# A fused attention and feed-forward kernel: the first k and q loads follow each other without gates, the first v load begins at once, the other early v loads get gates of their own, and fewer tiles are transposed on TensorE

## The chip, the cores and the metric

The kernel runs on one core of a Trainium2 chip. The metric is the device time of one execution in microseconds (us), and lower is better. A run is called slow when it is more than 1.5% above the fastest run of the same kernel; verdicts use fast runs alone. A trace is of one profiled execution, and its span is about 1.7 us shorter than the device time of the same run.

## The reference

```python
def _attn_ref(q, k, v, n_global, n_local):       # q, k, v: 4 batches x 8 heads x 768 x 64, float32
    ...
    keep = is_global | is_local                   # first 8 positions, or the last 96
    scores = scale * q @ k.T + bias[None]         # bias: -slope(head) * distance
    a = softmax over the kept positions
    return a @ v

def _moe_ref(x, w_in, w_out):                     # x: 3072 x 512, w_in: 512 x 2048, w_out: 2048 x 512
    h = x @ w_in
    g = h - np.tanh(h)
    return g @ w_out
```

The attention output is rearranged to x (3072 rows of 512) and goes through the feed-forward part. The result is 3072 x 512 in float32.

## The kernel before

The 3072 rows are 24 tiles of 128, numbered u = 0 to 23, six for each batch. For each tile the kernel loads k, q and v, transposes k and q (**T**), computes scores, exponentials and masks, multiplies by v (**AV**), normalizes (**x**), transposes x, and runs the first product (**m1**, with w_in), tanh, a subtraction, and the second product (**m2**, with w_out).

A small planner inside the kernel, at build time, gives each operation an assumed duration and picks, step by step, what can start first. What it emits is a fixed order for each engine. Changing an assumption or a gate therefore also changes the order of the instructions, on every engine. This matters below.

There are two roads for loads. GpSimd issues those that also convert to bf16: k and q of tiles 0 to 3 (128 KB each as written) and the eight pieces of the weights (512 KB each). These go through its ring (software queue). SyncE issues all v and the k and q of later tiles, as float32 (256 KB each), which an engine then casts. The DMA transposes of later tiles and the stores are also in SyncE's order.

```python
    PE_T, PE_X = 9, 9        # tiles below these are transposed on TensorE (k and q; x), others by DMA
    EARLY, EARLY2 = 9, 5
    ...
    def started(key, i):
        dmas[key] = i
        g = gate_of.get(key)
        if g is not None:            # a gate: issue this load only when load g has landed
            tc.add_manual_dep(i.ins, dmas[g].ins.name, ...)
    ...
    def load(u, nm, src, dst):
        ...
        if u < LB and nm != "vf":    # LB = 4
            started(("ld", nm, u), nc.gpsimd.dma_start(out=kq[u][...], in_=...))      # L161
        else:
            started(("ld", nm, u), nc.sync.dma_start(out=dst[u], in_=...))            # L166
    def load_w_in(j):
        started(("in", j), nc.gpsimd.dma_start(out=w_in_bf[j], ...))                  # L170
    def load_w_out(j):
        started(("out", j), nc.gpsimd.dma_start(out=w_out_bf[j], ...))                # L173
    ...
    def cast_v(u):                                                                    # L185
        nc.gpsimd.tensor_copy(out=vb[u % NV][:, :, 0:Dh], in_=vf.pop(u))
    ...
    AHEAD = 5.0              # how many tiles transposes may run ahead of m1
    before = [               # the order of loads: tiles ("t": k, q, v) and weight pieces
        ("t", 0), ("t", 1), ("t", 2), ("t", 3), ("in", 0), ("in", 1), ("in", 2), ("in", 3), ("out", 0),
        ("out", 1), ("out", 2), ("t", 4), ("out", 3), ("t", 5), ("t", 6), ("t", 7),
    ]
    ...
    for n, (key, ring, us) in enumerate(atoms):          # atoms: the single loads of that list
        if n and ring is not atoms[n - 1][1]:            # where the ring changes,
            due = at + 0.3 - T_LAND - T_ISSUE[ring]
            past = [x for e, x in ends if e <= due]
            if past:
                gate_of[key] = past[-1]                  # wait for the last load that is due by then
            elif key[1] == "vf":
                gate_of[key] = ("ld", "kf", key[2])
        at += us
        ends.append((at, key))
```

The gates that come out of this are: v0 after k0; v1 and k2 after q0; v2 and k3 after q1; v3 and w_in piece 0 after q2; k4 after w_out piece 1; w_out piece 3 after piece 2; k5 after v4.

The softmax here doesn't subtract the row's maximum and nothing guards it: scores larger than these inputs give would overflow.

Of the kernel before, what the change touches and what calls it, by code (L numbers as in the profile page):

```python
# [12 lines left out]
ENG = mybir.EngineType  # L13
# [3 lines left out]
def kernel(  # L17
# [11 lines left out]
    nc = tc.nc  # L29

    B, H, S, Dh = q.shape
# [15 lines left out]
    NV = 8  # L47
    PE_B = 4
    LB = 4
    PE_T, PE_X = 9, 9  # L50
    HT = 3


    EARLY, EARLY2 = 9, 5
    groups = [[u] for u in range(EARLY)] + [[u, u + 1, u + 2] for u in range(EARLY, NU, HT)]
    group_of = {u: g for g, us in enumerate(groups) for u in us}

# [22 lines left out]
    vb = [cpool.tile([P, H, Dh + 1], BF16, name=f"vb{i}") for i in range(NV)]  # L80
# [40 lines left out]
        nc.scalar.activation(mk[:, h, :, :], rmat, AF.Exp, bias=0.0, scale=-slope(h))  # L121


    ops = {}
    w_in_r = moe_w_in.rearrange("(c p) f -> p c f", p=P)
    w_out_r = moe_w_out.rearrange("(j p i) d -> j p i d", p=P, i=FJ)
    PE, ACT, DVE, POOL, SP = ENG.PE, ENG.Activation, ENG.DVE, ENG.Pool, ENG.SP

    LAT = {PE: 0.17, ACT: 0.1, DVE: 0.1, POOL: 0.12, SP: 0.0}

    def op(key, eng, us, fn, after=(), take=(), give=(), pri=0, dma=0.0):
        ops[key] = dict(
            key=key, eng=eng, us=us, fn=fn, after=[a for a in after if a is not None],
            take=list(take), give=list(give), pri=pri, dma=dma,
        )

    gate_of = {}
# [13 lines left out]
    kf, qf, vf = {}, {}, {}  # L151
# [23 lines left out]
    def cast(u, j, src):  # L175
        if u not in kq:
            kq[u] = bpool.tile([P, 2, H * Dh], BF16, name="kq")
        t = src.pop(u)
        nc.gpsimd.tensor_copy(  # L179
            out=kq[u][:, j, :].rearrange("p (c a d) -> p a c d", a=2, d=Dh),  # L180
            in_=t.rearrange("p (a c) d -> p a c d", a=2),
        )

    def cast_v(u):
        nc.gpsimd.tensor_copy(out=vb[u % NV][:, :, 0:Dh], in_=vf.pop(u))  # L185


    tr, qk, sc, pr, av, xs, xT = {}, {}, {}, {}, {}, {}, {}
# [121 lines left out]
    def shape1(g):  # L310
        n = len(groups[g]) * P
        return groups[g][0] // HT, groups[g][0] % HT * P, n, 512 // n
# [69 lines left out]
    def store(u):  # L382
        nc.sync.dma_start(out=out[u * P : (u + 1) * P, :], in_=ots.pop(u))


    AHEAD = 5.0
    WARM = (1.3, 13.0)
    BEGUN = {("ld", "kf", 0): 3.1, ("ld", "qf", 0): 3.8}
    T_LD, T_LD8, T_ST, T_DT, T_DX = 1.15, 0.75, 0.7, 1.75, 0.9
    T_W = {"in": 3.15, "out": 2.65}  # L390
    before = [
        ("t", 0), ("t", 1), ("t", 2), ("t", 3), ("in", 0), ("in", 1), ("in", 2), ("in", 3), ("out", 0),
        ("out", 1), ("out", 2), ("t", 4), ("out", 3), ("t", 5), ("t", 6), ("t", 7),
    ]


# [2 lines left out]
    T_LAND, T_ISSUE = 1.0, {SP: 1.6, POOL: 2.0}  # L399
    atoms = []  # L400
    for it in before:
        if it[0] == "t":
            u = it[1]
# [3 lines left out]
        else:  # L407
            atoms.append((it, POOL, T_W[it[0]]))
    at = 2.6
    ends = []  # L410
    for n, (key, ring, us) in enumerate(atoms):
        if n and ring is not atoms[n - 1][1]:
            due = at + 0.3 - T_LAND - T_ISSUE[ring]
            past = [x for e, x in ends if e <= due]
            if past:
                gate_of[key] = past[-1]
            elif key[1] == "vf":
                gate_of[key] = ("ld", "kf", key[2])
        at += us
        ends.append((at, key))  # L420
    for u in range(NU):
# [6 lines left out]
    for key, ring, us in atoms:  # L428
        gate = [gate_of.get(key), last.get(ring) and ("issue", last[ring])]
        if key[0] == "ld":  # L430
            nm, u = key[1:]
# [12 lines left out]
    for g, us in enumerate(groups):  # L444
        b, o, n, m = shape1(g)
# [7 lines left out]
    for u in range(NU):  # L453
        i = u % NQ
        if u >= LB:
            op(("ck", u), POOL, 0.62, lambda u=u: cast(u, 1, kf), after=[("ld", "kf", u)], take=["kq"], give=["kf"], pri=-1)
            op(("cq", u), POOL, 0.62, lambda u=u: cast(u, 0, qf), after=[("ld", "qf", u), ("ck", u)], give=["qf"], pri=-1)
        op(("cv", u), POOL, 0.62, lambda u=u: cast_v(u),
           after=[("ld", "vf", u), ("AV", u - NV + 1) if u >= NV else None,
                  ("V", (u - NV) // NQ * NQ + NQ - 2) if u >= NV else None], give=["vf"])  # L460
        go = [key for a, key in prog if a <= u - AHEAD]
        before_T = [("issue", ("T", u - 1)) if u else None, go[-1] if go else None]
# [41 lines left out]
    for g, us in enumerate(groups):  # L504
        b, o, n, m = shape1(g)
# [31 lines left out]
    def plan():  # L537
        bufs = {"big": 2, "one": 4, "mo": 3, "kf": 4, "qf": 4, "vf": 4, "kq": 4, "p0": 3, "p1": 3,
                "x": 3, "xT": 4, "g": 3, "th": 3, "ot": 4}
        avail = {n: [0.0] * c for n, c in bufs.items()}  # L540
        free = {PE: WARM[0], ACT: 4.9, DVE: 5.0, POOL: 3.3, SP: 0.7}
        avail["one"][0] = WARM[1]
        dma_free = 0.0
# [73 lines left out]
    def with_warm(order):  # L617
        pe = sorted(t for t, key in order if ops[key]["eng"] is PE)
        last = WARM[0]
        n = 0  # L620
        for t in pe:
            while True:
                us = 0.43 if last < 4.8 else 0.22
                if last + us + 0.08 > min(t, WARM[1]):
                    break
# [55 lines left out]
```

## Time and profile before

| | kernel before |
|---|---|
| device time, median of 3 (lowest to highest) | 221.76 us (220.97 to 223.07) |
| span of the profiled run | 221.1 us |
| TensorE work, counted at the spacings that the chain shows | 200.5 us |
| time lost on TensorE before 40 us, and after | 10.8 us, 6.0 us |
| eviction and store after the last matmul | 3.8 us |
| clock halved | once, 12.36 to 15.78 us |

The prediction shows how the work is counted and which lines carry it. "Time lost" is everything on TensorE's time line that is not this work: idle time, and the excess of matmuls at half the clock. The split at 40 us is mine; by then the start is over in both kernels. The last matmul's end is counted at the same spacings; by its recorded end the tail is 3.5 us, as the prediction has it.

One more view is used later. The DMA view of the kernel before, for 0 to 40 us in slices of 1 us, shows the busy share of the DMA engines in tenths; then comes the row of the table of stretches for the same 40 us (window, length, busy us of PE, PEld, DVE, ACT, POOL, clock, DMA share, GB/s):

```profile
DMA  0039989999999959999999999999999989299989
```

```profile
0.00:40.00 40.00, 36.84 (x556) 26.18 (x560) 21.47 (x55) 25.30 (x40) 14.11 (x29) 0.96 0.98 178
```

The reader is to see one short dip at 14 us and another at 34. The transfers are kept fed for nearly all of the first 40 us, at 178 GB/s.

### The profile page before, as it was taken

What the parts mean: (1) busy time and instruction counts of PE and PEld (TensorE: products, weight loads), DVE (VectorE), ACT (ScalarE), POOL (GpSimd) and SP (SyncE); (2) the same over time, 40 slices, a digit from 0 to 9 for tenths busy, and PEclk for the clock granted to TensorE, in tenths of its full rate; (3) what the DMA queues carried; (4) which work ended last, traced back from release to release, by engine and by line L of the source; (5) the groups of instructions that cost most, each with busy time, mean ns of one, the idle gap of its engine ahead of it and who ended that gap; (6) DMA issues with size and microseconds to landing.
All of it is one profiled execution on the core that took longest, in us unless ns stands there. A gap on an engine that the chain in (4) does not pass through costs nothing.

```text
span 221.1 us, 5458 instructions
## 1 busy us (share of the span) xinstructions
PE 211.7 (96%) x2208; PEld 137.7 (62%) x2233; DVE 128.7 (58%) x258; ACT 129.2 (58%) x209; POOL 56.6 (26%) x98
## 2 busy tenths in 40 slices
PE   7699999999999989999999999999999999999993
PEld 2356996557998767556655665566666655555552
DVE  6136773357899677525885767557767644444300
ACT  4467766575887675445766656558684554534320
POOL 6473003146174345332144423330000000000000
PEclk9969999999999999999999999999999999999999
DMA  4999998599999999999999999997124121001112
GB/s 59 206 174 207 213 209 174 129 226 251 209 215 213 177 185 236 198 227 215 214 221 220 220 182 209 244 227 154 24 63 96 49 71 47 14 35 50 47 50 94
DMA packets 98025, 34.56 MB, mean 156 GB/s; under 512 B 91216, under 2 KB 94544, under 8 KB 98000
## 3 DMA queue, kind: packets, MB, share of 16 engines
q1 hardware_dynamic: 94160, 28.98, 63.8%
q0 software_dynamic: 3840, 5.24, 14.0%
q8 instruction: 17, 0.28, 0.5%
q14 instruction: 8, 0.07, 0.1%
HBM read 27.26 MB, written 6.29 MB: 152 GB/s over the span
## 4 chain that ended last, share of the span: by engine, by line
PE 80%; DMA 14%; issue 1%; SPq 1%; POOL 1%; ACT 1%; DVE 0%; POOLq 0%; ACTq 0%
PE one L352 34%; PE one L325 31%; DMA kf<-in_k_dram 6%; PE big L242 5%; DMA qk<-kq 4%; DMA kq<-in_k_dram 3%; PE big L265 2%; PE big L269 2%; PE big L235 2%; PE one L364 2%; DMA kq<-in_q_dram 1%; PE one L194 1%; SPq L209 1%; PE one L201 1%; PE one L292 1%
## 5 line engine op out<-in xcount | busy, mean ns | idle before, releaser
L342 DVE TENSOR_TENSOR g<-one,th 128x384 bf16<-128x384 f32 (+1 forms) x116 | 67.5, 595 | 35.4 <-ACT th L336 32.7
L336 ACT ACTIVATE th<-one 128x384 f32<-128x384 f32 (+1 forms) x116 | 60.6, 526 | 44.5 <-PE one L325 43.1
L352 PEld LDWEIGHTS <-g 128*128 128x128 bf16 x368 | 34.2, 98 | 33.8
L250 ACT ACTIVATE pd<-big 128x1024 bf16<-128x1024 f32 x24 | 24.6, 1023 | 12.8 <-PE big L242 12.8
L325 PE MATMUL one<-xT,w_in_bf_100 128*128 128x128 bf16 (+1 forms) x224 | 25.3, 258 | 0.0
L325 PE MATMUL one<-xT,w_in_bf_99 128*128 128x128 bf16 (+1 forms) x224 | 24.9, 258 | 0.0
L325 PE MATMUL one<-xT,w_in_bf_97 128*128 128x128 bf16 (+1 forms) x224 | 24.5, 258 | 0.0
L325 PE MATMUL one<-xT,w_in_bf_98 128*128 128x128 bf16 (+1 forms) x224 | 24.2, 258 | 0.1
L179 POOL CAST kq<-kf 128x512 bf16<-128x512 f32 x20 | 13.6, 680 | 40.5 <-DMA kf<-in_k_dram 40.1
L380 ACT COPY ot<-one 128x512 f32<-128x512 f32 x23 | 13.5, 587 | 17.1 <-PE one L352 16.9
L352 PE MATMUL one<-w_out_bf_101,g 128*128 128x512 bf16 x85 | 22.8, 379 | 0.5 <-issue 0.2
L352 PE MATMUL one<-w_out_bf_102,g 128*128 128x512 bf16 x88 | 22.9, 380 | 0.2
L250 ACT ACTIVATE po<-big 128x1024 bf16<-128x1024 f32 x20 | 20.5, 1024 | 4.1 <-PE big L242 4.1
L352 PE MATMUL one<-w_out_bf_104,g 128*128 128x512 bf16 x87 | 22.4, 379 | 0.3
L352 PE MATMUL one<-w_out_bf_103,g 128*128 128x512 bf16 x84 | 22.1, 380 | 0.3
L325 PEld LDWEIGHTS <-w_in_bf_99 128*128 128x128 bf16 x224 | 17.5, 114 | 5.7
L325 PEld LDWEIGHTS <-w_in_bf_98 128*128 128x128 bf16 x224 | 17.6, 114 | 5.3
L254 DVE TENSOR_TENSOR pd<-pd,mk 128x1024 bf16<-128x1024 bf16 x20 | 15.1, 756 | 9.5 <-ACT pd L250 9.5
L325 PEld LDWEIGHTS <-w_in_bf_97 128*128 128x128 bf16 x224 | 17.3, 114 | 5.0
L325 PEld LDWEIGHTS <-w_in_bf_100 128*128 128x128 bf16 x224 | 17.0, 114 | 5.3
L242 PEld LDWEIGHTS <-qk 64*128 64x128 bf16 x352 | 10.0, 95 | 11.9 <-issue 8.6
L242 PE MATMUL big<-qk 64*128 64x128 bf16 x352 | 16.1, 220 | 1.2 <-DMA qk<-kq 1.0
(108 smaller groups left out, 199.0 us busy)
## 6 DMA issues: line engine op xcount, KB each, us to landing
vf<-in_v_dram SPq DMA_DIRECT2D x24, 256.0 KB, 5.0
out_dram<-ot SPq DMA_DIRECT2D x23, 256.0 KB, 2.9
kf<-in_k_dram SPq DMA_DIRECT2D x20, 256.0 KB, 3.8
qf<-in_q_dram SPq DMA_DIRECT2D x20, 256.0 KB, 4.6
kq<-in_k_dram POOLq DMA_DIRECT2D x4, 128.0 KB, 4.8
kq<-in_q_dram POOLq DMA_DIRECT2D x4, 128.0 KB, 5.1
w_in_bf_97<-in_moe_w_in_dram POOLq DMA_DIRECT2D x1, 512.0 KB, 5.4
w_in_bf_98<-in_moe_w_in_dram POOLq DMA_DIRECT2D x1, 512.0 KB, 7.2
```

What stands on the lines that cost most here:

```text
L179: nc.gpsimd.tensor_copy(out=kq[u][:, j, :].rearrange("p (c a d) -> p a c d", a=2, d=Dh), in_=t.rearrange("p (a c) d -> p a c d", a=2),)
L235: nc.tensor.matmul(s[:, a * NP : (a + 1) * NP, :], ident, bm[:, a * NP : (a + 1) * NP, m, :], start=True, stop=False,)
L242: nc.tensor.matmul(s[:, hh * NP + p, :], qk[u - o][r, 1, p, :], qk[u][r, 0, p, :], start=(u >= PE_B), stop=(u >= PE_B or p == NP - 1),)
L250: nc.scalar.activation(pr[u, o], s, AF.Exp, bias=0.0, scale=scale)
L254: nc.vector.tensor_tensor(out=pr[u, o], in0=pr[u, o], in1=mk[:, :, m, :], op=ALU.mult)
L265: nc.tensor.matmul(dst, pr[u, 0][:, h, :], vb[u % NV][:, h, :], start=True, stop=last,)
L269: nc.tensor.matmul(dst, pr[u, 1][:, h, :], vb[(u - 1) % NV][:, h, :], start=False, stop=True,)
L325: nc.tensor.matmul(t[:, (f - f0) * n : (f - f0 + 1) * n], w_in_bf[j][:, c, i : FJ * P : FJ], xT[b][:, c, o : o + n], start=(c == 0), stop= ...
L336: nc.scalar.activation(h_view(ths[g, f0], g), h_view(hs[g, f0], g), AF.Tanh, bias=0.0, scale=1.0)
L342: nc.vector.tensor_tensor(out=gs[b][:, f0 : f0 + m, o : o + n], in0=h_view(hs.pop((g, f0)), g), in1=h_view(ths.pop((g, f0)), g), op=ALU.su ...
L352: nc.tensor.matmul(os_[u], gs[u // HT][:, f, t * P : (t + 1) * P], w_out_bf[f // FJ][:, f % FJ, :], start=(f == 0), stop=(f == CF - 1),)
L380: nc.scalar.copy(out=ots[u], in_=os_.pop(u))
```

## The change

The intent is to let GpSimd issue its first loads back to back, to begin the first v in the empty first microseconds, to bring w_in piece 0 forward, and to leave fewer transposes to TensorE. The diff, cut to its core:

```diff
-    PE_T, PE_X = 9, 9
+    PE_T, PE_X = 8, 5
-    EARLY, EARLY2 = 9, 5
+    EARLY, EARLY2 = 9, 3
-    def cast_v(u):
-        nc.gpsimd.tensor_copy(out=vb[u % NV][:, :, 0:Dh], in_=vf.pop(u))
+    def cast_v(u, e=POOL):
+        (nc.vector if e is DVE else nc.gpsimd).tensor_copy(out=vb[u % NV][:, :, 0:Dh], in_=vf.pop(u))
-    AHEAD = 5.0
-    WARM = (1.3, 13.0)
+    AHEAD = 6.0
+    WARM = (1.3, 15.0)
-    T_LD, T_LD8, T_ST, T_DT, T_DX = 1.15, 0.75, 0.7, 1.75, 0.9
-    T_W = {"in": 3.15, "out": 2.65}
+    T_LD, T_LD8, T_ST, T_DT, T_DX = 1.1, 0.65, 0.7, 1.75, 0.9
+    T_W = {"in": 2.6, "out": 2.6}
     before = [
-        ("t", 0), ("t", 1), ("t", 2), ("t", 3), ("in", 0), ("in", 1), ("in", 2), ("in", 3), ("out", 0),
-        ("out", 1), ("out", 2), ("t", 4), ("out", 3), ("t", 5), ("t", 6), ("t", 7),
+        ("t", 0), ("t", 1), ("t", 2), ("in", 0), ("t", 3), ("in", 1), ("t", 4), ("in", 2), ("in", 3),
+        ("t", 5), ("out", 0), ("out", 1), ("out", 2), ("out", 3), ("t", 6), ("t", 7),
     ]
...
-    for n, (key, ring, us) in enumerate(atoms):
-        if n and ring is not atoms[n - 1][1]:
-            ...
+    by = None
+    for key, ring, us in atoms:
+        beside = key[:2] == ("ld", "vf") and key[2] < LB
+        if beside and key[2]:
+            gate_of[key] = ("ld", "vf", 0) if key[2] == 1 else ("ld", "kf", key[2] - 2)
+        elif not beside:
+            if by not in (None, ring):
+                ...                      # the gate as before, over the loads that are not "beside"
+            by = ring
...
-        op(("cv", u), POOL, 0.62, lambda u=u: cast_v(u),
+        op(("cv", u), (DVE, POOL) if u < LB else (POOL,), (0.48, 0.62) if u < LB else (0.62,), lambda e, u=u: cast_v(u, e),
```

The gates after the change are: v0 none; v1 after v0; v2 after k0; v3 after k1; k4 after v3; w_in piece 2 after piece 1; k5 after w_in piece 2; w_out piece 0 after w_in piece 3; k6 after w_out piece 2. GpSimd's ring holds k0, q0, k1, q1, k2, q2, w_in 0, k3, q3, w_in 1 with no gate among them. `T_LD` to `T_W` are the planner's assumed times of transfers. `WARM` bounds the stretch in which the planner fills idle time of TensorE with warm-up multiplications of zeros.

More of the change, by code (lines that the diff above doesn't have):

```diff
@@ L121, in mask @@
         nc.scalar.activation(mk[:, h, :, :], rmat, AF.Exp, bias=0.0, scale=-slope(h))
+    PE, ACT, DVE, POOL, SP = ENG.PE, ENG.Activation, ENG.DVE, ENG.Pool, ENG.SP
     ops = {}
@@ L126 @@
     w_out_r = moe_w_out.rearrange("(j p i) d -> j p i d", p=P, i=FJ)
-    PE, ACT, DVE, POOL, SP = ENG.PE, ENG.Activation, ENG.DVE, ENG.Pool, ENG.SP
     LAT = {PE: 0.17, ACT: 0.1, DVE: 0.1, POOL: 0.12, SP: 0.0}
@@ L410 @@
     ends = []
-    for n, (key, ring, us) in enumerate(atoms):
-        if n and ring is not atoms[n - 1][1]:
-            due = at + 0.3 - T_LAND - T_ISSUE[ring]
-            past = [x for e, x in ends if e <= due]
-            if past:
-                gate_of[key] = past[-1]
-            elif key[1] == "vf":
-                gate_of[key] = ("ld", "kf", key[2])
+    by = None
[5 more added lines that the diff above has]
+            if by not in (None, ring):
+                due = at + 0.3 - T_LAND - T_ISSUE[ring]
+                past = [x for e, x in ends if e <= due]
+                if past:
+                    gate_of[key] = past[-1]
+            by = ring
         at += us
```

## The prediction

> **What bounds the kernel now.** I read four views of the profile: the page, then the chain of waits, then the table of stretches, then the timelines of TensorE and GpSimd over the first 36 us. On the page TensorE is busy nearly throughout, DMA works at its limit to about slice 28, and the clock row has one dip:
>
> ```profile
> PE 211.7 (96%) x2208; PEld 137.7 (62%) x2233; DVE 128.7 (58%) x258; ACT 129.2 (58%) x209; POOL 56.6 (26%) x98
> ...
> PEclk9969999999999999999999999999999999999999
> DMA  4999998599999999999999999997124121001112
> ```
>
> Busy is not useful, so I count TensorE's work from spacings that the chain shows. Sixteen 128-wide first-product matmuls (L325) take 0.89 us, four 384-wide ones 0.65, four of the second product (L352) 0.86, sixteen scores (L242) 0.55, a pair of bias matmuls (L235) 0.43, sixteen 64-wide transposes (L201) 0.44, eight wide transposes (L194) 0.45, four of x (L292) 0.22, the last 32 (L364) 3.5, and AV 0.031 each. With the program's counts (576, 320, 368, 352, 14, 128, 40, 36, 32, 352) this is 32.0+51.9+79.3+12.1+3.0+3.5+2.2+2.0+3.5+10.9 = **200.4 us**. The trace shows only 344 of the 368 L352 matmuls; I use the program's count. The last matmul ends at 217.5, so 17.1 us are lost on TensorE, and 3.5 us of eviction and store follow to 221.1.
>
> When is it lost? The first L325 starts at 20.07. Before it there are 128 L201, 12 L235, 48 L242, 40 AV and 8 L292, that is 3.5+2.6+1.65+1.25+0.45 = 9.4 us of work. So **10.7 us are lost before 20.07 and 6.4 us in the 197 us after**. The chain of waits names the early loss:
>
> ```profile
> 2.01 3.02 DMA kq<-in_q_dram
> 5.03 0.28 issue
> 5.32 5.54 DMA kq<-in_k_dram
> 10.90 0.44 PE one L201 x16
> ```
>
> The reader sees k of tile 2 issued only once q of tile 0 landed (5.03: a gate), then 5.54 us of transfer, and TensorE starting on it at 10.90. The GpSimd timeline shows the two gates inside the ring:
>
> ```profile
> 5.32 0.51 POOL L161 DMA_DIRECT2D kq<-in_k_dram  x1 [1.18 <-DMA kq<-in_q_dram]
> ...
> 8.20 0.52 POOL L161 DMA_DIRECT2D kq<-in_k_dram  x1 [1.85 <-DMA kq<-in_q_dram]
> ```
>
> The table of stretches (columns: window and length; busy us of PE, PEld, DVE, ACT, POOL; then clock, DMA share, GB/s) shows what the hole did:
>
> ```profile
> 5.00:10.00 5.00, 4.00 (x78) 2.17 (x75) 0.69 (x1) 2.67 (x4) 2.69 (x5) 1.00 1.05 189
> 10.00:15.00 5.00, 4.10 (x65) 2.44 (x66) 1.75 (x4) 2.19 (x3) 2.81 (x4) 0.74 1.00 180
> 15.00:20.00 5.00, 4.98 (x96) 2.79 (x96) 2.53 (x7) 3.92 (x5) 3.60 (x7) 0.92 1.21 200
> ```
>
> From 12.36 to 15.78 the clock was halved, right after TensorE idled 8.96 to 10.90. Note also that DMA is already busy from 5 us: removing gates mostly reorders transfers rather than filling an idle DMA.
>
> **What the Trainium skill says.** (1) "TensorE: Matmul & The Clock Gate", Part 1, says an idle activity window of about 3.4 us drops the clock to half. The trace agrees on size (one dip of 3.41 us at 0.5), though 1.94 us idle within a window was enough. (2) "DMA: Bandwidth & Descriptors", Issuing engines are not separate DMA queues: transfers from GpSimd and SyncE interleave on the same 16 engines. The trace agrees: v of tile 0, moving while GpSimd's ring was mostly empty, took 1.3 us from first to last packet; v of tiles 1 and 2, beside k and q, took 2.5 and 2.7; v of tile 4, beside a w_out piece, took 5.1. (3) Same page, Anatomy of one DMA: a fixed cost of about 2 us. The trace's first k took 3.07 us from issue to landing with packets moving for only 1.16. (4) The clock-gate page's architectural detail says VectorE is strict FIFO; this matters for the moved v casts, and no run so far tests it here.
>
> **The change, part by part.**
>
> *Less TensorE work.* PE_T 9 to 8 takes 8 wide transposes away, 8 x 0.056 = 0.45 us; PE_X 9 to 5 takes 16 x transposes, 0.90 us. The instruction order shows the score groups in 18 single and 13 double runs, where 26 and 9 were before: four joins. A single run takes 0.33 and a double 0.55 in the chain, so a join saves 0.11, together 0.44. All of this lies on the bounding engine: **-1.8 us**. In exchange DMA gets one more qk and four more x transposes. A recorded qk transpose moves packets for 1.0 to 1.4 us when undisturbed and an x one for 0.7, so 1.2 + 4 x 0.7 = 4 us of DMA in the 50 to 90 us region, where DMA is full. But tile 5 now loads before w_out, and AHEAD 6 lets transposes go further ahead, so I count this as zero.
>
> *The first loads.* In the new order GpSimd issues k1, q1, k2, q2, w_in piece 0, k3, q3, w_in piece 1 without a landing gate; at about 0.5 us an issue k2 goes out at 4.1 (5.32 before). v0 goes out at about 0.8 instead of 4.44, and uses DMA before the first k's packets at 2.72; it should land near 4 to 5, and may delay k0 by 0.3. A k or q piece takes about 0.7 us of packets when alone (128 KB at some 180 KB/us) and 1.3 to 1.7 beside a v. I work it out serially: q1 done near 7.3, k2 8.6, q2 10.0, plus about 0.8 to landing: k2 lands near 9.4 (10.86), q2 10.8 (11.76). w_in piece 0 follows and lands near 14 (18.15), but k3 and q3 stand behind it: near 15.7 and 17 (13.72, 14.50). v1 lands near 8.5 (12.14), v2 near 11 (13.86), v3 near 13.6.
>
> *What TensorE makes of it.* T(2) starts 1.5 us earlier and the 2 us hole shrinks, so the halved clock (1.7 us lost, half of 3.41) probably does not return whole. But the order then has m1 of tile 0 ahead of AV(1), T(3) behind k3 and q3, and the second quarter of m1 behind w_in piece 1, near 20. By 20.4 I count 3.5 (T) + 2.15 (bias) + 1.4 (scores) + 1.25 (AV) + 0.45 (x) + 1.8 (two m1 quarters) = 10.5 us done, so 9.9 lost instead of 10.7: **-0.8 us**.
>
> *The v casts of tiles 0 to 3 on VectorE.* 4 x about 0.48 (the planner's figure) where GpSimd took 0.61 to 0.71. GpSimd is then free to issue; VectorE was busy 2.44 of 10 us from 5 to 15. The work is hidden, but cast 2 stands ahead of the first normalization, so a late v2 holds x(0).
>
> *Order and gates after 20 us.* w_in pieces 2 and 3 wait for piece 1 to land, tile 5 for piece 2, w_out for piece 3. GpSimd's order has cast v5 between cast k5 and cast q5, so T(5) waits for v5, which moves beside w_out as v4 did. I allow **+1.0 us**. The other stalls after 20 us (6.4, among them 0.96 at 81.2 and 0.42 at 108.8 behind qk transposes) fall by a guess of 1.6 with more slack: **-1.6**.
>
> *Sum.* -1.8 - 0.8 + 1.0 - 1.6 = -3.2 us on a profiled 221.1, which gives 217.9, and as a median **218.5**.
>
> **The rivals.** *A: transfers only change places.* DMA moves the same bytes and was busy from 5 us (share 1.05, 1.00, 1.21); what k2 and w_in piece 0 gain, k3, q3 and v pay. For it: v's slow progress beside k and q. Against it: in the first 2.5 us nothing moved, and v0 fills that. Then only the 1.8 us of work goes: about 220. *B: a new wait takes the gate's place:* v1 or v2 crawls behind an ungated GpSimd ring, and VectorE's in-order casts hold the score evictions and x(0), or T(5) waits for v5; two idle windows, each halving the clock. For it: 5.1 us for v4 beside a large transfer. Against it: v1 starts 1 us or more earlier than it did. Then 221 to 223. *C: the planner's timing fits the chip,* no dip, start loss near 8.5, late stalls near 4: 200.4-1.8+8.5+4+3.5 = 214.6, so about 215.3.
>
> **Range and chances.** The start's sum can be off by 1.5 us and the late stalls by 1.5 to 2, so about 2.5 to 3 together: 215.5 to 221.5. Faster by over 2% needs 217.3 or less, 1.2 us better than my sum: 0.32. Slower by over 2% needs 226.2, beyond all but a bad case of B: 0.05. Within 2%: 0.63.
>
> **What would show it right or wrong.** v0 issued before 1 us; k2's T at 9 to 10 and not 10.9; w_in piece 0 landed by 15; k3 later than 13.7; 24 fewer transposes on TensorE; a clock row with no dip or a lesser one before 20 us; first L325 near 14 to 15; a wait for w_in piece 1 near 19 to 20; a wait for T(5) in the 30s. I am wrong if TensorE waits more than 2 us on VectorE's v casts, if the tile-5 wait exceeds 2 us, or if fewer stalls after 20 us bring more than 3 us.

## The result, and the profile after

| | before | after |
|---|---|---|
| device time, median | 221.37 us (4 runs, 220.67 to 223.07) | **228.77 us** (4 runs, 228.65 to 231.32) |
| ratio of fast runs [95%] | | **1.035** [1.027, 1.043] |
| span of the profiled run | 221.1 us | 229.6 us |
| TensorE work | 200.5 us | 199.2 us |
| lost before 40 us | 10.8 us | **21.0 us** |
| lost after 40 us | 6.0 us | 5.8 us |
| clock halved | 3.4 us | 10.2 us |

A ratio here is the mean time of one kernel's fast runs over the mean of the other's in the same rounds, so it is not quite the ratio of the quoted medians. All runs in this table are fast ones. The profiled run of the changed kernel was its slowest; the spans of the four others were 226.8 to 227.5 us, so some 2 us of its loss belong to that run alone; where they lie isn't known. The changed kernel is 3.5% slower, and the profile puts the whole loss into the first 40 us.

The page of the changed kernel, with the lines that answer to those of the kernel before:

```profile
PE 213.0 (93%) x2206; PEld 136.4 (59%) x2206; DVE 129.0 (56%) x259; ACT 125.6 (55%) x205; POOL 54.5 (24%) x95
...
PEclk9795899999999999999999999999999999999999
DMA  6993994999998999999989999998932210111112
```

The share of TensorE is down from 96% to 93%, and the clock row dips twice, in slices 2 and 4. There is also a hole in the DMA row, in slice 4. The DMA view for 0 to 40 us in 1 us slices shows the holes plainly, and the row of the stretches gives their sum:

```profile
DMA  0099998999999999998300059999999998891017
```

```profile
0.00:40.00 40.00, 29.01 (x431) 18.73 (x432) 17.74 (x53) 18.27 (x25) 13.50 (x30) 0.87 0.87 149
```

DMA starts a microsecond earlier than before, as intended, but stands almost still from 19 to 23 us and from 36 to 39. By 40 us it has moved 149 x 40 = 6.0 MB instead of 178 x 40 = 7.1. The stretches that answer to those in the prediction, and two more:

```profile
10.00:15.00 5.00, 3.35 (x68) 1.79 (x64) 1.03 (x2) 2.54 (x3) 0.21 (x1) 0.86 1.23 207
15.00:20.00 5.00, 0.33 (x4) 0.33 (x5) 1.62 (x4) 0.00 (x0) 0.00 (x0) 0.82 0.96 157
20.00:25.00 5.00, 5.00 (x43) 2.94 (x42) 1.15 (x4) 2.05 (x2) 1.50 (x2) 0.50 0.37 70
...
35.00:40.00 5.00, 5.00 (x101) 4.63 (x99) 3.89 (x9) 3.98 (x6) 2.75 (x6) 1.00 0.41 77
```

From 15 to 20 us the engines are idle for most of the time while DMA is busy (0.96). From 20 to 25 us it is the other way round: TensorE runs at half its clock, and DMA moves 70 GB/s. TensorE's timeline names the wait, and VectorE's timeline names what stands behind it (start, duration, what; in brackets the idle time before it and what ended it):

```profile
13.06 0.44 PE L201 MATMUL one<-ident,kq 128*64 128x64 bf16 x16
19.68 0.61 PE L292 MATMUL one<-ident,x 128*128 128x128 bf16 x4 [6.17 <-DVE x L278]
...
23.12 1.89 PE L325 MATMUL one<-xT,w_in_bf_97 128*128 128x128 bf16 x16
```

```profile
18.35 0.43 DVE L185 CAST vb_107<-vf 128x512 bf16<-128x512 f32 x1 [5.67 <-DMA vf<-in_v_dram]
18.69 0.20 DVE L277 RECIPROCAL rden<-big 128x8 f32<-128x8 f32 x1
18.93 0.69 DVE L278 TENSOR_TENSOR x<-big,rden 128x512 bf16<-128x512 f32 x1
```

TensorE waits 6.17 us for x of tile 0. The normalization that makes x is ready to run but stands behind the cast of v2 in VectorE's order, and that cast waits 5.67 us for v2 to land. After that idle time the clock was halved from 18.21 to 25.03: the first sixteen matmuls of m1 take 1.89 us, where 1.06 was recorded before. The wait (6.17), half of the 5.35 us that TensorE then worked at half the clock (2.7), and one more wait, for q4 (1.48 us, until 33.89), add up to 10.3 us, about the 10.2 by which the start got longer. The other halved stretch, 7.97 to 11.38, takes the place of the one before; it follows waits of 0.71, 0.21 and 0.72 us for k0, q0 and k1, which landed up to 1 us later than before. The chain of waits shows what v means for the loads:

```profile
7.78 13.97 DMA vf<-in_v_dram
...
21.77 5.56 DMA kf<-in_k_dram
...
27.99 5.21 issue
```

v3 is 14 us on its way, and k4 is issued only when it has landed (its gate). The 5.21 us of issue end when q4, which landed at 33.17, is cast. Landing times, predicted and measured:

| load | before | predicted | after |
|---|---|---|---|
| v0 | 8.75 | 4 to 5 | 3.80 |
| k2, q2 | 10.86, 11.76 | 9.4, 10.8 | 10.36, 11.21 |
| v1 | 12.14 | 8.5 | 11.63 |
| v2 | 13.86 | 11 | **18.32** |
| v3 | 15.21 | 13.6 | **21.75** |
| w_in 0, w_in 1 | 18.15, 20.70 | 14, 20 | 16.49, 21.25 |
| k3, q3 | 13.72, 14.50 | 15.7, 17 | 17.04, 17.91 |
| w_in 2, w_in 3 | 24.08, 26.63 | not given | 28.04, 32.61 |
| w_out 0 | 29.71 | not given | 42.54 |

Why v2 and v3 take so long can be read from the DMA view of the changed kernel for 13 to 18 us. It counts, for GpSimd's ring (software) and for SyncE's queue (hardware), packets, MB, and the share of the time of 16 engines:

```profile
q0 software_dynamic: 793, 0.76, 90.1%
q1 hardware_dynamic: 800, 0.20, 30.4%
```

Both got nearly the same number of packets (as the profile counts them), but a packet of the ring held 0.96 KB on average and one of v 0.25 KB. So v moved at 40 KB/us beside w_in. At that rate a v of 256 KB takes 6.4 us of packets (an estimate from the second line), and the prediction had taken 2.5 to 2.7. The same stretch of e1, e2, e4 and e6 below, which have the ring without gates too, shows the same: 783 packets against 814, 794 against 795, 780 against 798, 769 against 768.

The GpSimd timeline shows the ring without gates up to 7.1 us, and then what the later gates do:

```profile
4.14 0.56 POOL L161 DMA_DIRECT2D kq<-in_k_dram  x1
...
7.12 0.82 POOL L170 DMA_DIRECT2D w_in_bf_98<-in_moe_w_in_dram  x1
21.53 0.76 POOL L170 DMA_DIRECT2D w_in_bf_99<-in_moe_w_in_dram  x1 [8.04 <-DMA w_in_bf_98<-in_moe_w_in_dram]
...
37.46 0.55 POOL L173 DMA_DIRECT2D w_out_bf_101<-in_moe_w_out_dram  x1 [0.29 <-issue]
```

Ten loads are in the ring by 7.9 us; before, k3 was not issued until 8.20 and w_in 0 not until 12.75. Then w_in 2 waits for w_in 1, which lands at 21.25, half a microsecond from v3, which gates the SyncE side. For a moment both roads are empty at once. That is the hole at 19 to 23. The hole at 36 to 39 is another: w_in 3 landed at 32.61, but the issue of w_out 0 stands in GpSimd's order behind two casts and two copies, the last of which waits 2.02 us for VectorE, until 37.46.

### The profile page after: what moved, and what is told of

The parts are those of the page before. It is cut to its first block, busy times and chain, and to the rows that moved or that the text cites. A ratio compares the mean times of both kernels' runs of the same rounds, so it can differ in the third digit from the quotient of the medians.

```text
span 229.6 us, 5437 instructions
## 1 busy us (share of the span) xinstructions
PE 213.0 (93%) x2206; PEld 136.4 (59%) x2206; DVE 129.0 (56%) x259; ACT 125.6 (55%) x205; POOL 54.5 (24%) x95
## 4 chain that ended last, share of the span: by engine, by line
PE 64%; DMA 25%; issue 3%; SPq 3%; POOL 1%; DVE 1%; ACT 1%; POOLq 0%; DVEq 0%
PE one L325 29%; PE one L352 26%; DMA qk<-kq 12%; DMA vf<-in_v_dram 6%; DMA kf<-in_k_dram 5%; PE big L242 4%; SPq L166 2%; DMA kq<-in_k_dram 2%; PE one L364 2%; PE big L265 1%; PE big L269 1%; SPq L304 1%; PE one L194 1%; ACT th L336 1%; POOL kq L179 1%
## 5 line engine op out<-in xcount | busy, mean ns | idle before, releaser
L179 POOL CAST kq<-kf 128x512 bf16<-128x512 f32 x20 | 14.3, 717 | 62.0 <-DMA kf<-in_k_dram 59.9
L325 PE MATMUL one<-xT,w_in_bf_97 128*128 128x128 bf16 (+1 forms) x224 | 26.0, 264 | 0.2 <-DVE xT L217 0.2
L325 PE MATMUL one<-xT,w_in_bf_98 128*128 128x128 bf16 (+1 forms) x224 | 25.6, 258 | 0.0
L325 PE MATMUL one<-xT,w_in_bf_100 128*128 128x128 bf16 (+1 forms) x224 | 25.6, 258 | 0.0
L325 PE MATMUL one<-xT,w_in_bf_99 128*128 128x128 bf16 (+1 forms) x224 | 25.3, 258 | 0.0
L250 ACT ACTIVATE po<-big 128x1024 bf16<-128x1024 f32 x20 | 20.5, 1023 | 8.6 <-PE big L242 8.5
L352 PE MATMUL one<-w_out_bf_102,g 128*128 128x512 bf16 x92 | 23.6, 379 | 0.0
L352 PE MATMUL one<-w_out_bf_101,g 128*128 128x512 bf16 x92 | 23.5, 379 | 0.0
L352 PE MATMUL one<-w_out_bf_103,g 128*128 128x512 bf16 x92 | 23.5, 379 | 0.0
L352 PE MATMUL one<-w_out_bf_104,g 128*128 128x512 bf16 x92 | 23.5, 379 | 0.0
L254 DVE TENSOR_TENSOR pd<-pd,mk 128x1024 bf16<-128x1024 bf16 x20 | 14.4, 719 | 14.1 <-ACT pd L250 13.6
L325 PEld LDWEIGHTS <-w_in_bf_97 128*128 128x128 bf16 x224 | 18.2, 116 | 6.0 <-issue 0.5
L325 PEld LDWEIGHTS <-w_in_bf_98 128*128 128x128 bf16 x224 | 17.4, 114 | 5.6
L325 PEld LDWEIGHTS <-w_in_bf_99 128*128 128x128 bf16 x224 | 17.3, 114 | 5.6
L325 PEld LDWEIGHTS <-w_in_bf_100 128*128 128x128 bf16 x224 | 17.2, 114 | 5.6
L242 PEld LDWEIGHTS <-qk 64*128 64x128 bf16 x352 | 10.3, 96 | 14.5 <-issue 7.4
```

The lines of the kernel that those rows point to most:

```text
L179: nc.gpsimd.tensor_copy(out=kq[u][:, j, :].rearrange("p (c a d) -> p a c d", a=2, d=Dh), in_=t.rearrange("p (a c) d -> p a c d", a=2),)
L242: nc.tensor.matmul(s[:, hh * NP + p, :], qk[u - o][r, 1, p, :], qk[u][r, 0, p, :], start=(u >= PE_B), stop=(u >= PE_B or p == NP - 1),)
L250: nc.scalar.activation(pr[u, o], s, AF.Exp, bias=0.0, scale=scale)
L254: nc.vector.tensor_tensor(out=pr[u, o], in0=pr[u, o], in1=mk[:, :, m, :], op=ALU.mult)
L325: nc.tensor.matmul(t[:, (f - f0) * n : (f - f0 + 1) * n], w_in_bf[j][:, c, i : FJ * P : FJ], xT[b][:, c, o : o + n], start=(c == 0), stop= ...
L352: nc.tensor.matmul(os_[u], gs[u // HT][:, f, t * P : (t + 1) * P], w_out_bf[f // FJ][:, f % FJ, :], start=(f == 0), stop=(f == CF - 1),)
```

## The experiments

Fourteen kernels were run, all correct and in four groups; each group shares a chip and the runs of the kernel before (its median was 221.62 to 221.88 in them). More than twelve were used because the prediction was wrong and two questions were still open then. Of the theories that the texts on record name, the **in-order cast** is the first: VectorE's wait for v2 is the loss, and the start would be good without it. **Starved loads** is the second: SyncE's v loads crawl because GpSimd's ring is never empty beside them, and everything gated on v is late. The texts from e9 on call these T1 and T2, and set a T3 against T2: the DMA is simply full, and what is held back costs as much as it gives. What is left over is the last: the new order of the loads, or the part of the change outside the start, is what costs.

The time lost on TensorE, before and after 40 us, is given for each from its profiled run, by the same count as above. A profiled run is one run; medians and ratios decide. How rough these two columns are can be seen from e13: over 14 runs it equals the kernel before, and yet the columns differ by 1.8 and 0.8 us. The profiled run of the kernel before (222.83 us, with 3.4 us at half clock) lay 1.5 us above its median, that of e13 (220.15 us, with none) 1.6 us below. So differences of up to 2 us in them say little.

| run | median us | ratio [95%] | lost <40 us | lost >40 us |
|---|---|---|---|---|
| before | 221.37 | 1 | 10.8 | 6.0 |
| after | 228.77 | 1.0349 [1.0269, 1.0429] | 21.0 | 5.8 |
| e1 v casts later in the order | 230.92 | 1.0406 [1.0347, 1.0465] | 20.7 | 4.4 |
| e2 v casts on GpSimd | 225.52 | 1.0179 [1.0108, 1.0249] | 15.6 | 5.2 |
| e9 w_in held for v | 226.31 | 1.0225 [1.0141, 1.0309] | 14.9 | 6.3 |
| e5 old gate rule | 228.33 | 1.0294 [1.0213, 1.0374] | 14.6 | 9.3 |
| e6 old list of loads | 228.69 | 1.0230 [1.0135, 1.0324] | 18.1 | 6.9 |
| e12 old list, w_in 0 held | 229.17 | 1.0339 [1.0288, 1.0390] | 12.9 | 11.0 |
| e4 before, with the new start | 231.15 | 1.0408 [1.0332, 1.0483] | 20.5 | 4.5 |
| e3 after, with the old start | 227.06 | 1.0231 [1.0165, 1.0296] | 9.1 | 11.8 |
| e7 e3 with the old transposes on TensorE | 225.46 | 1.0143 [1.0049, 1.0237] | 9.2 | 8.8 |
| e8 e3 with the old AHEAD and EARLY2 | 226.80 | 1.0243 [1.0167, 1.0318] | 9.3 | 10.8 |
| e11 before, v0 at once | 224.43 | 1.0089 [1.0058, 1.0120] | 10.1 | 7.1 |
| e10 before, v0 at once and no gates on k and q | 223.61 | 1.0063 [1.0031, 1.0095] | 10.3 | 8.7 |
| e13 as e11, same order of instructions | 221.74 | 1.0002 [0.9971, 1.0033] | 9.0 | 5.2 |
| e14 as e10, same order of instructions | 222.85 | 1.0055 [1.0032, 1.0078] | 9.3 | 7.6 |

The median is over all runs, the ratio over fast runs. Only e6, e7, e10, e11, e13 and e14 had slow runs, and the kernel before had one to four in every group but the first; for e6, with two of its four runs slow, the median says little. With 9 of e11's 20 runs and 6 of e10's above the line of 1.5%, their ratios of fast runs are at the low end: over all runs, means give 1.013 and 1.010.

### Taking the cast out of the way: e1 and e2

e1 leaves the transfers and the engines of the casts as they are and moves the casts of v1, v2 and v3 behind the work that they held up.

```diff
     order, model_end = plan()
+    at_of = {key: t for t, key in order}
+    later = {("cv", 1): ("Te", 1, 0), ("cv", 2): ("Xe", 0), ("cv", 3): ("Xe", 2)}
+    order = sorted(((at_of[later[key]] + 1e-6 if key in later else t, key) for t, key in order), key=lambda x: x[0])
```

> The changed kernel, with one difference: on VectorE the casts of v1, v2, v3 stand later in the order, each just ahead of where its own tile needs it, so that the first normalization no longer stands behind a v that has not landed (v2 landed at 18.32). Transfers as in the changed kernel. Theory T1, the in-order wait on VectorE is the cost: x(0) goes through at about 14 instead of 19.7, the 6.2 us of TensorE idleness vanish with the halved clock after it, and the time falls from 228.7 by 6 us or more, to 222.7 or less. Theory T2, the late landings themselves are the cost: TensorE only moves its wait to w_in piece 0 (landed 16.5), q3 (17.9), v2 (18.3), later q4 (33.2); the time falls by 3 us at most, to 225.7 or more.

Measured: 230.92 us, no gain. The wait for x(0) is gone (its transposes ran at 14.93 instead of 19.68), but TensorE's timeline in e1 shows two others in its place:

```profile
28.22 0.46 PE L194 MATMUL one<-ident,kq 128*128 128x128 bf16 x4 [3.25 <-POOL kq L179]
...
32.11 0.61 PE L194 MATMUL one<-ident,kq 128*128 128x128 bf16 x4 [3.44 <-POOL kq L179]
```

These are the transposes of tile 4. v3 landed at 20.75 here, k4 is gated on it and landed at 27.49, and q4, beside w_in 2 and w_in 3, landed at 31.39. The clock was halved for 13.7 us. The in-order cast is where the delay met TensorE; it isn't the delay. As the sole cause it is rejected.

e2 puts the casts of tiles 0 to 3 back on GpSimd, and the planner then makes a new order.

```diff
-        op(("cv", u), (DVE, POOL) if u < LB else (POOL,), (0.48, 0.62) if u < LB else (0.62,), lambda e, u=u: cast_v(u, e),
+        op(("cv", u), (POOL,), (0.62,), lambda e, u=u: cast_v(u, e),
```

> The changed kernel with only the part undone that lets the casts of v0 to v3 run on VectorE: they are on GpSimd again, ahead of the issue of w_in piece 2. T1: as good as the run with the later casts, 222.7 or less, since VectorE no longer waits for v; w_in piece 2 is issued after v3's landing (21.75) instead of 21.5, about the same. T2: 225.7 or more. If the choice of engine as such mattered, this and the run with later casts would differ by more than 2 us.

Measured: 225.52 us, 3.3 us better than the changed kernel and still 4 us worse than before. v2 and v3 landed nearly as late (16.83, 20.95), but k4 landed at 24.18, because w_in 2 went out a little after k4 instead of before it. The two waits for tile 4 are then 1.1 and 1.8 us:

```profile
PE one L194 <- POOL kq L179: 2.9, 2, 1.8
```

The median lies between what T1 and T2 had said, just under T2's 225.7, and e1 and e2 differ by 5.4 us, more than the 2 that were to tell of the engine. So the engine of the casts is worth some microseconds, at least in part through a different order of issue; the two aren't separated. The start still loses 15.6 us.

### Feeding SyncE's loads: e9

e9 keeps all of the change, with two gates more. w_in 0 goes out only after v2 has landed, and w_in 1 after v3.

```diff
+    gate_of["in", 0] = ("ld", "vf", 2)
+    gate_of["in", 1] = ("ld", "vf", 3)
     for u in range(NU):
```

> The changed kernel with two gates put back into GpSimd's ring: w_in piece 0 waits for v2 to land, w_in piece 1 for v3. k3 and q3 stand behind piece 0 as in the changed kernel. The casts stay on VectorE in the planner's order. Theory T2 (SyncE's loads get little of the DMA while GpSimd's ring always holds more work, so v and k4 land late and TensorE waits for them in one place or the next): v2 lands near 13 instead of 18.3, v3 near 17 instead of 21.75, k4 and q4 near 21 and 24 instead of 27.3 and 33.2; TensorE's wait at x(0) falls from 6.2 to about 1 us, that at T(4) below 1; time 222 to 225. Rival T3 (the DMA is simply full: what is held back costs as much as it gives): v2 and v3 land no earlier than 16 and 20, or w_in pieces 0 and 1 land over 4 us later than 16.5 and 21.3 and TensorE waits for those; time 228 or more.

Measured: 226.31 us, 2.5 better than the changed kernel, but 1.3 above the range of T2; the intervals of the two ratios overlap a little, so the landings carry the argument and not the time. The time from issue to landing of the four early v, as the view of the tile gives it for the kernel after and then for e9:

```profile
DMA to landing us min/median/max: 3.1/10.4/14.0
```

```profile
DMA to landing us min/median/max: 3.1/6.2/7.2
```

v2 landed at 11.98 and v3 at 12.70, where they had landed at 18.32 and 21.75. The clock was 1.000 over the profiled span, against 0.978. The two groups of waits of TensorE in e9 that matter (total, times, longest):

```profile
PE one L325 <- DMA w_in_bf<-in_moe_w_in_dram: 2.7, 4, 1.8
...
PE one L292 <- DVE x L278: 0.4, 1, 0.4
```

The wait for x(0) fell from 6.2 to 0.4 us although the casts stand on VectorE in this kernel too. This shows that the full ring starves SyncE's loads, and that this, not the place of the cast, opens the wait for x(0). The size varies: in the four kernels with these gates and this list (after, e1, e2, e4) v2 landed at 15.06 to 18.32 and v3 at 20.42 to 21.75, and e9 lies well below both. T3 is rejected for the early loads: w_in 0 and 1 landed at 18.43 and 24.05, only 1.9 and 2.8 us later, where it had asked for over 4. What remains of the start, 14.9 against 10.8 us, is partly w_in: its last two pieces landed at 29.68 and 33.41. So the starving is shown as the cause of the late v, and not as the cause of all 7.4 us.

### The old gates or the old list: e5, e6 and e12

e5 has the old rule for gates, with the new list of loads; its diff is the reverse of the gate part of the change. e6 has the new rule with the old list.

```diff
-        ("t", 0), ("t", 1), ("t", 2), ("in", 0), ("t", 3), ("in", 1), ("t", 4), ("in", 2), ("in", 3),
-        ("t", 5), ("out", 0), ("out", 1), ("out", 2), ("out", 3), ("t", 6), ("t", 7),
+        ("t", 0), ("t", 1), ("t", 2), ("t", 3), ("in", 0), ("in", 1), ("in", 2), ("in", 3), ("out", 0),
+        ("out", 1), ("out", 2), ("t", 4), ("out", 3), ("t", 5), ("t", 6), ("t", 7),
```

> The changed kernel with only the rule of the gates undone: v0 waits for k0, k2 for q0, v1 for q0, v2 and w_in piece 0 for q1, v3 and w_in piece 1 for v2. The order of the loads, the casts on VectorE, the rest stay. T2 says that the gate of w_in piece 1 on v2 is what helps (v2 beside one piece of weights and not two), while v0 comes 4 us later than with the new rule: v3 lands near 19, time 224 to 227. T3: 228 or more.

> The changed kernel with only the order of the loads undone: tile 3 ahead of w_in, then all of w_in and three pieces of w_out in a row without gates, then tile 4. k3 and q3 land near 12 and 13 instead of 17 and 17.9; v2 and v3 still crawl beside the ring (v2 near 14 to 16, v3 near 18 to 20), but nothing of tile 4 waits for v3 and x(0) waits for v2 alone. T2: TensorE's wait at x(0) is 2 to 4 us, there is none at T(4) before 36; time 223 to 226. If the order of the loads is not a cause, 228 to 229.

Measured: e5 228.33 us; e6 228.69 us with two slow runs, 1.023 by the fast ones. With e5 the start loses 14.6 us, one wait being 2.0 us for w_in 2, which landed at 29.34; the time after 40 us loses 9.3. v3 came at 18.25, as T2 had said (near 19), and the start gained, but the time is T3's (228 or more): the late waits took the gain. With e6 v2 and v3 are as late as after the change, or later (19.09, 25.68), and TensorE waits 5.3 us for x(0) (in a slow run): the list alone does not mend the starving. Its two fast runs, 226.38 and 227.59, lie between its two expectations and settle nothing about the list.

e12 puts the two remedies together: the old list, and w_in 0 held for v2.

```diff
     before = [
-        (the new list)
+        (the old list)
     ]
...
+    gate_of["in", 0] = ("ld", "vf", 2)
     for u in range(NU):
```

> The changed kernel with the old order of the loads and w_in piece 0 held until v2 has landed (the held run and the old-order run joined). If both named causes are right (v crawls beside an ungated ring of weights; w_in pieces 2 and 3 come too late in the new order), TensorE's waits at x(0) and for w_in fall under 1 us each, the start loses about what it lost before (10 to 11 us by 40 us), and the time is 221 to 224.5, what remains being waits near 100 us as in the runs with the old start. If the order of the loads is no cause, it stays at 226 like the held run.

Measured: 229.17 us, which no theory had foreseen. Against e6 it has one gate more, and v2 and v3 come 5.4 and 11.1 us earlier (13.72, 14.59): the starving is shown a second time. The start is nearly mended (w_in 3 at 28.16, 12.9 us lost; the wait for x(0) is still 1.5 us), but the time after 40 us loses 11.0 us. Its two largest groups of waits, from 40 to 160 us:

```profile
PE big L242 <- DMA qk<-kq: 3.7, 5, 1.2
...
PE one L325 <- DMA xT<-x: 2.4, 3, 1.6
```

These are waits for DMA transposes of k and q and of x. So a good start is followed by late waits, which the next runs separate.

### The start against the rest: e3, e4, e7 and e8

The start is the list, the gates, the planner's times of loads, `WARM`, and the place of the v casts. The rest is PE_T and PE_X, EARLY2, and AHEAD. e3 is the changed kernel with the old start, and e4 the changed kernel with the old rest.

```diff
 e3:
-    WARM = (1.3, 15.0)
+    WARM = (1.3, 13.0)
-    T_LD, T_LD8, ... = 1.1, 0.65, ...     and T_W, the list, the gates and the cast of v: all as before
+    T_LD, T_LD8, ... = 1.15, 0.75, ...
 e4:
-    PE_T, PE_X = 8, 5
+    PE_T, PE_X = 9, 9
-    EARLY, EARLY2 = 9, 3
+    EARLY, EARLY2 = 9, 5
-    AHEAD = 6.0
+    AHEAD = 5.0
```

> The start of the kernel before (order and gates of the loads, casts of v on GpSimd, the planner's transfer times, warm matmuls to 13 us), with the rest of the change: 8 and 5 tiles transposed on TensorE, 3 tiles of the second product ahead, and 6.0 tiles of lookahead. If the whole loss comes from the start, as the two traces say (21 us lost by 40 us, 10.9 before), this keeps the start's 10.9 and brings the savings after: 1.8 us of work and about 1.6 us of stalls, so about 218. If the rest of the change also costs, it is 221 or more.

> The complement: the new start (loads, gates, casts, transfer times) with 9 and 9 tiles transposed on TensorE, 5 tiles ahead and lookahead 5.0 as before. If the start costs about 10 us and the rest saves about 3, this is the slowest of all, about 231. If the two do not add up, because the planner orders the start otherwise, it is 227 to 229.

Measured, as medians in us:

| | old start | new start |
|---|---|---|
| old rest | 221.62 (before) | 231.15 (e4) |
| new rest | 227.06 (e3) | 228.77 (after, from another group) |

The new start costs 9.5 us with the old rest, but only 1.7 with the new one. The rest costs 5.4 us where the start is on time, and saves 2.4 where the start is late. The parts do not add up. The chain of waits of e3 near 95 us shows what the rest costs:

```profile
92.26 0.70 DVE x L278
92.96 0.34 SPq L304
...
93.42 3.36 DMA kf<-in_k_dram
...
96.90 0.62 POOL kq L179
```

SyncE has the DMA transpose of x (L304) ahead of a k load in its order. That transpose waits for VectorE's normalization until 92.96. Only then is k issued, at 93.42; it lands 3.36 us later, is cast, and its own DMA transpose follows. TensorE waits 2.69 us for that, until 99.87.

e7 and e8 take one half of the rest back each, on top of e3: e7 has PE_T and PE_X at 9 and 9, e8 has AHEAD 5 and EARLY2 5.

```diff
 e7, on e3:
-    PE_T, PE_X = 8, 5
+    PE_T, PE_X = 9, 9
 e8, on e3:
-    EARLY, EARLY2 = 9, 3
+    EARLY, EARLY2 = 9, 5
-    AHEAD = 6.0
+    AHEAD = 5.0
```

> The kernel before with only the lookahead 6.0 (5.0) and 3 tiles of the second product ahead (5); 9 and 9 tiles are transposed on TensorE as before, loads as before. It halves the run that kept the old start with the rest of the change (227.1, with waits of 2.9 and 1.7 us at 97 and 100 us behind a qk and an x transpose on SyncE's queue). If the five transposes that were moved to SyncE's queue are what costs, this stays at 220.5 to 222.5, the one with the moved transposes alone goes to 225 or more. If lookahead and early tiles cost, this is at 225 or more and the other near 220.

> The other half: the kernel before with only 8 and 5 tiles transposed on TensorE (9 and 9); lookahead and early tiles as before. My prediction's step (1.35 us of TensorE work saved, the five transposes free on the DMA) would give 220.2. If the transposes delay the loads on SyncE's queue and TensorE runs out of scores between 85 and 110 us, 224 or more.

Measured: e7 225.46 us (1.014), e8 226.80 us (1.024). Each half alone costs something with the old start (3.8 and 5.2 us by the medians, together more than the 5.4 of both at once), so neither fork of the two expectations holds alone. The largest late waits, first of e7 and then of e8:

```profile
PE one L325 <- DMA xT<-x: 3.2, 1, 3.2
```

```profile
PE big L242 <- DMA qk<-kq: 3.1, 1, 3.1
```

They end at 103.39 and 98.91 us. With the new start, TensorE reaches that place some 12 us later (21.0 us lost before 40 us, against 9.1 in e3) and the transposes are there: the largest single loss after 40 us in the changed kernel is 0.88 us. It is in this sense that the late start hides the cost of the rest; the table shows that it does, while the reason is read from traces, and no run delays the start alone.

### The gates alone: e10, e11, e13 and e14

e11 is the kernel before with one gate dropped: v0 goes at once. e10 also drops the gates of k2 and k3, so that k and q follow each other.

```diff
 e11:
+    gate_of.pop(("ld", "vf", 0), None)
     for u in range(NU):
 e10:
+    for key in [("ld", nm, u) for u in range(LB) for nm in ("kf", "qf")] + [("ld", "vf", 0)]:
+        gate_of.pop(key, None)
     for u in range(NU):
```

> The kernel before with one gate less: v0 no longer waits for k0 to land. It lands near 3.8 instead of 8.75, in time in which nothing moved, and may delay k0 by 0.8 us (5.2 to 5.4 landed, as in the changed kernel, against 4.42). If this part of the change is sound by itself, 220 to 222; if the later k0 is what counts, 222.5 or more.

> The kernel before with only these gates taken away: those of k2, q2, k3, q3 in GpSimd's ring and that of v0; w_in piece 0 still waits for q2, v1 for q0, v2 for q1, v3 for q2; casts on GpSimd; all other parameters as before. T2: k2 lands near 9.5 instead of 10.9 and T(2) starts 1.4 us sooner, v1 to v3 come at 12 to 17, w_in piece 0 at 16 to 17; the dip of the clock goes or shrinks; time 218.5 to 221 against 221.5. T3, or if a full DMA gives nothing back: 221 to 223. If ungated k and q by themselves are the harm: 225 or more.

Measured over 20 runs each: 1.0089 [1.0058, 1.0120] and 1.0063 [1.0031, 1.0095]. Neither gains: e10 misses the 218.5 to 221 that T2 gave it, and e11 looks like the case in which a later k0 counts. But the planner knows the gates, so both kernels also have another order of instructions. e13 and e14 drop the same gates only where the wait is emitted. The plan, and so every engine's order, is that of the kernel before.

```diff
 e13:
-        if g is not None:
+        if g is not None and key != ("ld", "vf", 0):
 e14:
-        if g is not None:
+        if g is not None and key not in (("ld", "vf", 0), ("ld", "kf", 2), ("ld", "kf", 3)):
```

> The kernel before, instruction order on every engine unchanged, with the one wait of v0's load on k0's landing dropped from the program. If the planner's new order was the cost of the earlier v0 (224.4 with a new order, waits near 115 us), this is 221 to 222, equal to before within 0.5%. If the transfers are the cost (k0 lands 0.9 us later), it is 222.5 or more.

> The kernel before, instruction order unchanged, without the waits of v0 on k0, of k2 on q0 and of k3 on q1: the first q and k rows follow each other in GpSimd's ring. w_in piece 0 still waits for q2. New-order theory: k2 lands near 9.6 and the first stretch gains up to 1 us, time 219.5 to 221.5 (before 221.6). Transfer theory: 222.5 or more, with v1 to v3 late and a wait of TensorE on AV or x in the first 20 us.

Measured: e13 1.0002 [0.9971, 1.0033] over 14 runs, e14 1.0055 [1.0032, 1.0078] over 22. So v0 at once is worth nothing by itself: it landed at 3.73 instead of 8.75 and k0 0.8 us later. The 0.9% of e11 came from its new order; the same gate is dropped in both. For the gates in the ring it is the other way round: 0.55 of 0.63% remain with the order unchanged, so the moved loads make that loss. In e14 k2 landed 2.2 us earlier than before (8.66), but v1 did not (12.15 for 12.14), and w_in 0 is still gated on q2. TensorE is further along at 18 us, and there meets the cast of v2, which stands in GpSimd's order behind seven issues of weights. The waits of TensorE in e14, first for 0 to 40 us, then for 40 to 160:

```profile
PE big L265 <- POOL vb L185: 1.3, 1, 1.3
```

```profile
PE big L242 <- DMA qk<-kq: 1.0, 2, 0.9
PE one L194 <- POOL kq L179: 1.0, 1, 1.0
```

The number of the transfer theory came true (222.5 or more), and its wait on AV, but not its late v (12.15, 13.29 and 15.02 for v1 to v3, no later than before). By the count of one run each, e14 loses 0.3 us more than e13 before 40 us and 2.4 us more after, which is hardly more than two runs of equal kernels differ by. What is shown is that the earlier k bought nothing, and that at 18 us something else, in a fixed order, was next.

No variant beats the kernel before; e13 equals it.

## Why the prediction was wrong

The prediction's sum was -3.2 us on the span. Measured on the two profiled spans it is +8.5:

| term | predicted | measured |
|---|---|---|
| less TensorE work | -1.8 | -1.35 |
| the start (-0.8), with tile 5 and v5 (+1.0) | +0.2 | +10.2 |
| stalls later | -1.6 | -0.2 |
| sum | -3.2 | +8.65 (the tail is about 0.2 shorter, which gives 8.5) |

- **Less work.** The 24 transposes went as stated, for 1.35 us. The four joins of score groups (0.44) are not resolved by this count. The changed kernel against e4 shows the whole rest to be worth 2.4 us behind the late start.
- **The first loads: this step failed.** The prediction had "v1 lands near 8.5 (12.14), v2 near 11 (13.86), v3 near 13.6". The landings were 11.63, 18.32 and 21.75. I took the rate of a v beside k and q from the kernel before, 2.5 and 2.7 us of packets. But there the gates left the ring empty between k and q pairs, and w_in was not there yet. Beside a ring with w_in in it, a v moved at 40 KB/us, which makes 6.4 us of packets, and v2 landed 6.7 us after v1. e9, which keeps w_in out of the ring until v2 has landed, gives v2 at 11.98 and v3 at 12.70, close to what the prediction said: its rate holds for a ring without w_in. Only v1 was mis-timed there as well (11.02 for 8.5). k2 at 10.36 was 1 us later than said, but w_in 0 (16.49 for 14), k3 and q3 were late by 1 to 2.5 us only. It was the share between the two roads that I had wrong.
- **What TensorE makes of it.** "-0.8 us" became +10.2. T(2) started at 11.33, later than the 10.90 of before: k2 had landed at 10.36, but two warm-up matmuls, at half the clock from 10.37, stood ahead of it. The first L325 came at 23.12 instead of near 14 to 15. k0 was 1 us later beside v0, not 0.3. The half-clock stretches added instead of going: 10.2 us against 3.4.
- **The v casts on VectorE.** "cast 2 stands ahead of the first normalization, so a late v2 holds x(0)" is what happened, and I gave it no cost in the sum. The wait of 6.17 us is also the first of the signs by which I had said I would be wrong (more than 2 us). e1 shows that it is not the root.
- **Order and gates after 20 us.** The +1.0 us for T(5) and v5 was wrong in its place: v5 landed at 36.80 and T(5) ran at 44.67 without a wait. The gates cost elsewhere: k4 behind v3, and two holes in the transfers.
- **DMA transposes counted as zero.** With the late start this held. e3, e7 and e8 show that it does not hold when the start is on time.
- **Rivals.** A does not fit: by 40 us 1.1 MB less had been moved, so the transfers did not only change places. C, with no dip of the clock and less lost at the start, does not fit either. B, which had part of the 0.05 that I gave to a slower kernel, "v1 or v2 crawls behind an ungated GpSimd ring", was the right mechanism, but its "221 to 223" was too small by 6 us, and what spoke against it ("v1 starts 1 us or more earlier") said when v is issued, not how it is served. It also did not count what is gated on v: k4, and through it tile 4.

**What stays open.** e12 mends the start to within 2 us of before and still needs 229.17 us. Its groups of waits for DMA transposes sum to 6.1 us of the 11.0 lost late; the remainder is spread. By the count it loses no more late than e3 (11.8) and 3.8 us more early; why a start that is nearly mended should bring late waits of that size is not settled. Why the planner's new orders in e10 and e11 are worse is only seen (e11 has extra waits of AV on masks near 115 us), not explained. Neither hole in the transfers was tested by itself. While k and q stood in the ring beside w_in (6 to 12 us of the changed kernel), it got 690 packets against 1824 of SyncE's queue; why v fared better there than from 13 us on is not settled. A run that takes the gate of k4 off v3 and changes nothing else was not made.

## What to carry to other kernels

A gate that looks like lost time on one queue may be what gives another queue its share: before taking it away, ask which loads move in the hole that it leaves, and what is gated on them. In a kernel whose order comes from a planner, test a gate with the order of instructions held fixed, else two changes are measured as one. And do not add the worth of a later part to that of an earlier one: a start that is late hides later waits, and a start that is on time pays them.

## What the Trainium skill lacked or had wrong

- "DMA: Bandwidth & Descriptors", Issuing engines are not separate DMA queues, says that transfers of different issuers interleave, and gives no number for their shares. Queues, rings and completion order on the same page says that each engine takes turns between its queues by packets; what that does to the bytes isn't said. Here, from 13 to 18 us, the ring with w_in and SyncE's queue with v got 793 and 800 packets, as the profile counts them, but 0.76 and 0.20 MB. A 256 KB load issued by SyncE took 3.1 us from issue to landing when nearly alone, and 12.9 and 14.0 us (v2 and v3, part of it behind the one before) beside that ring; with w_in held back, at most 7.2 us.
- "TensorE: Matmul & The Clock Gate", Part 1, ties the halved clock to an idle window of about 3.4 us. In the kernel before, one recorded idle time of 1.74 us (9.16 to 10.90; the prediction has 1.94) was followed by 3.4 us at half clock. Its length alone does not decide: after 1.75 us in e9 (until 33.45) and 3.24 us in e7 (until 103.39) there was none. How much idle time within a window is enough isn't said there, and no run here shows it.
- Neither lacking nor wrong: the same page's architectural detail on VectorE's strict FIFO held. A cast that waited 5.67 us kept a normalization, ready to run, behind it.
- No page that I found gives the cost of placing a load behind a DMA transpose in SyncE's order. In e3 a k load was issued at 93.42 us, when the transpose ahead of it had waited for VectorE until 92.96, and TensorE waited for the result.
